# Loading all 128 partitions of every item in a chunked-attention stage, padding rows included

## The chip, the cores and the metric

The kernel runs on one core of one Trainium2 chip. The metric is the device time of one execution in microseconds (us). A single execution scatters by about 1% in these runs, so kernels are compared by the runs that were made side by side on one chip. Ratios are the mean time of one kernel's fast runs over the mean of the other's fast runs of the same rounds, with a 95% interval; so they are not quite the ratio of the medians quoted beside them. "Faster" or "slower" is given from 2% on, with the whole interval beyond it; a smaller difference whose interval leaves out 1 is called clear of noise.

## The reference

An attention stage (RWKV-5, 4 batches, 8 heads, 768 tokens, head dimension 48) is followed by a mixture of 8 experts:

```python
# attention: a running state per head
for t in range(S):
    y[:, :, t] = r_t @ (state + (u * k_t) outer v_t)
    state = w * state + k_t outer v_t
# experts: every token goes to one expert e (its own best, or that of the token before)
h = np.maximum(x[b, s] @ w1[e], 0.0)
out[b, s] = p[e] * (h @ w2[e])
```

All is fp32. The change touches only how the attention stage loads r, k and v.

## The kernel before: the parts that matter

The attention stage works through 16 items, one per batch and pair of heads. The tile `rk` holds r and k of both heads with the head dimension on the partitions: 48 rows of the first head, 16 rows of zeros, 48 rows of the second head, 16 rows of zeros. `vT` is laid out in the same way. `kv` holds tokens on the partitions and uses all 128 of them. Four sets of buffers take turns:

```python
NB = 4
ROWS = DP + DH                    # 64 + 48 = 112: the last 16 rows are zeros
...
def load(n):
    b, hp = divmod(n, HP)
    rk, vT, kv = rks[n % NB], vTs[n % NB], kvs[n % NB]
    q = slice(0, P if n < NB else ROWS)
    nc.sync.dma_start(out=rk[q].rearrange("p a c t -> p (a c t)"), in_=rk_d[b, hp, q])
    nc.sync.dma_start(out=kv, in_=kv_d[b, hp])
    nc.sync.dma_start(out=vT[q].rearrange("p a c t -> p (a c t)"), in_=vT_d[b, hp, q])
```

The first four items load every row, so that the padding in each buffer is zero once and for all; from item 4 on only rows 0 to 111 are loaded. The loop that uses them (cut; each helper issues the work of one item on several engines):

```python
for n in range(M + 2):
    if n + 2 < M:
        load(n + 2)
    turn(n - 2, ...)       # transposes tp, one item starts here on TensorE
    added(n); scale(n + 1) # VectorE kw, GpSimd ke, pd, rw; matmuls T
    inside(n - 1)          # matmuls yp, the last use of kv
    ...
    own(n); scores(n, 0); scores(n, 1)   # matmuls dp, sc
```

After every fourth item x is stored, and small matmuls for the expert logits (lp, then lq, called the gather) are added.

## Time and profile before

| | before |
|---|---|
| median of the runs beside the first comparison | 510.37 us (508.65 to 510.77, 4 runs) |
| profiled execution | 509.2 us |
| attention ends (last transposes tp start) | 137.08 us |
| TensorE idle between 25 and 125 us | 7.3 us, six times |
| time at half clock inside attention | 52.6 to 62.9 us |

The first three rows come from the runs and from the timeline of TensorE, the last two from the timeline and from the clock records. The prediction below shows the lines of the profile that carry its argument. One word on their reading: TensorE counts as busy from the start of a matmul to its modelled end. What tells of a lost microsecond is therefore the last column of the timeline, the idle before an instruction. "issue" there means that no semaphore explains the idle. Three words are used throughout: "the ring" stands for the loads that have been asked for and have not landed; a "block" is 256 instructions of TensorE in a row; a "crossing" is the start of the first instruction of a block.

### The profile page before, as it was taken

Reading aid. Unit: us, or ns where it says so; the run is one execution under the profiler, and the core shown is the slowest. Engines: PE = TensorE matmul, PEld = TensorE weight load, DVE = VectorE, ACT = ScalarE, POOL = GpSimd, SP = SyncE. Lnnn points to the kernel's source line nnn. Section 1 sums busy time; section 2 is a strip of 40 time slices with the busy share of each in tenths; the row PEclk is TensorE's granted clock in tenths of the full one; section 3 lists DMA queues with packets and bytes.
Section 4 is the critical chain, followed back from the end, with each engine's and each line's share of the span. In section 5 each row is a group of like instructions: output and inputs, shape, how many; then the busy total and the mean of one; then the engine's idle time right before and its main releaser. Section 6 shows DMA issues by size and latency. Waiting matters only on the chain.

```text
span 509.2 us, 8106 instructions
## 1 busy us (share of the span) xinstructions
PE 453.5 (89%) x3470; PEld 281.7 (55%) x3470; DVE 149.4 (29%) x243; ACT 73.0 (14%) x180; POOL 149.2 (29%) x133
## 2 busy tenths in 40 slices
PE   3989799899833589999999999999999999999980
PEld 2977598798623545555555555555555555555540
DVE  7776357566357010111110110111111111111020
ACT  2122122222200001011011110110111111011010
POOL 6876377482011250211311212212212202001111
PEclk9999599999965579999999999999999999999995
DMA  8999968841094130071071071071161152000001
GB/s 317 359 248 249 319 188 281 231 149 70 15 382 194 31 109 0 23 279 46 27 279 43 24 274 46 24 257 69 31 240 75 32 198 83 16 0 32 9 10 49
DMA packets 16525, 67.53 MB, mean 133 GB/s; under 512 B 2887, under 2 KB 6250, under 8 KB 14432
## 3 DMA queue, kind: packets, MB, share of 16 engines
q1 hardware_dynamic: 9504, 51.98, 30.3%
q0 software_dynamic: 3840, 10.23, 6.2%
q10 hardware_dynamic: 3136, 4.72, 2.7%
q8 instruction: 29, 0.48, 0.4%
q14 instruction: 16, 0.13, 0.1%
HBM read 57.48 MB, written 10.22 MB: 133 GB/s over the span
## 4 chain that ended last, share of the span: by engine, by line
issue 56%; PE 25%; POOL 13%; DMA 2%; POOLq 1%; DVE 1%; ACT 0%; SPq 0%
POOL out_dram L610 6%; PE sc L183 6%; POOL xg L566 5%; PE yp L194 5%; PE tp L216 3%; PE T L143 3%; PE dp L166 2%; PE mp L527 2%; PE T L154 2%; PE yp L204 2%; PE lp L227 1%; DMA x_d<-x 1%; DMA rk<-in_rk_dram 1%; PE lq L235 1%; DMA xg<-x_d,gid 1%
## 5 line engine op out<-in xcount | busy, mean ns | idle before, releaser
L594 PE MATMUL y<-hT,w2t 128*128 128x448 f32 x384 | 155.4, 541 | 0.0
L584 PE MATMUL h<-exT,w1t 128*128 128x448 f32 x384 | 155.0, 543 | 0.0
L584 PEld LDWEIGHTS h<-exT,w1t 128*128 128x128 f32 x384 | 71.9, 192 | 64.3 <-issue 64.3
L594 PEld LDWEIGHTS y<-hT,w2t 128*128 128x128 f32 x384 | 70.2, 190 | 58.8 <-issue 58.3
L610 POOL DMA_INDIRECT out_dram<-yo,sid x32 | 31.3, 978 | 174.6 <-DVE yo L608 174.0
L587 ACT ACTIVATE hT<-h 128x448 f32<-128x448 f32 x64 | 34.8, 544 | 284.8 <-PE h L584 284.8
L566 POOL DMA_INDIRECT xg<-x_d,gid x32 | 32.4, 1013 | 100.8 <-PE etp L578 84.7
L579 DVE COPY exT<-etp 128x384 f32<-128x384 f32 (+1 forms) x32 | 16.2, 508 | 131.9 <-PE etp L578 131.1
L608 DVE TENSOR_SCALAR yo<-otp,gate 128x384 f32<-128x384 f32 (+1 forms) x32 | 19.5, 615 | 118.7 <-PE otp L606 118.6
L183 PE MATMUL sc<-rw,kw 48*64 48x128 f32 x768 | 36.8, 292 | 2.7 <-issue 2.7
L127 POOL TENSOR_TENSOR ke<-kv,endT 128x576 f32<-128x576 f32 x16 | 26.1, 1634 | 27.1 <-DMA kv<-in_kv_dram 13.8
L183 PEld LDWEIGHTS sc<-rw,kw 48*64 48x64 f32 x768 | 31.0, 143 | 3.6 <-issue 3.5
L154 PE MATMUL T<-S,wd 48*64 48x64 f32 x256 | 30.3, 239 | 1.3 <-issue 1.1
L185 DVE TENSOR_TENSOR am<-sc,mask 128x768 f32<-128x768 f32 x32 | 29.3, 951 | 4.2 <-PE sc L183 3.8
L154 PEld LDWEIGHTS T<-S,wd 48*64 48x64 f32 x256 | 24.3, 143 | 6.8 <-issue 4.0
L129 POOL TENSOR_TENSOR pd<-rk 128x768 f32<-128x768 f32 x15 | 27.3, 1822 | 2.2 <-issue 2.2
L207 DVE TENSOR_TENSOR xT<-yp,own 128x768 f32<-128x768 f32 x16 | 15.3, 958 | 39.1 <-PE yp L204 39.1
L166 PE MATMUL dp<-pd,w_t 48*64 48x384 f32 x128 | 22.4, 521 | 4.7 <-issue 3.0
L130 POOL TENSOR_TENSOR rw<-rk,pw 128x768 f32<-128x768 f32 x15 | 25.3, 1688 | 3.3 <-PE yp L204 3.3
L194 PE MATMUL yp<-am,kv 128*64 128x128 f32 x384 | 26.2, 283 | 0.0
L578 PEld LDWEIGHTS etp<-ident,xg 128*128 128x128 f32 (+1 forms) x96 | 11.9, 150 | 21.9 <-issue 19.8
L156 ACT COPY S<-T 128x64 f32<-128x64 f32 x64 | 13.6, 213 | 71.0 <-PE T L154 71.0
(138 smaller groups left out, 312.5 us busy)
## 6 DMA issues: line engine op xcount, KB each, us to landing
w1t<-in_w_dram SPq DMA_DIRECT2D x8, 1536.0 KB, 6.3
w2t<-in_w_dram SPq DMA_DIRECT2D x8, 1536.0 KB, 7.6
kv<-in_kv_dram SPq DMA_DIRECT2D x16, 584.0 KB, 8.0
rk<-in_rk_dram SPq DMA_DIRECT2D x12, 672.0 KB, 10.4
x_d<-x ACTq DMA_DIRECT2D x4, 1152.0 KB, 6.0
vT<-in_vT_dram SPq DMA_DIRECT2D x12, 336.0 KB, 7.3
rk<-in_rk_dram SPq DMA_DIRECT2D x4, 768.0 KB, 8.4
vT<-in_vT_dram SPq DMA_DIRECT2D x4, 384.0 KB, 9.1
```

The source lines that it names most:

```text
L127: nc.gpsimd.tensor_mul(t["ke"], t["k"], spread(endT[:, hp].rearrange("p i d -> p (i d)"), 1, NCH))
L129: nc.gpsimd.tensor_mul(t["pd"], t["rT"], t["kT"])
L154: nc.tensor.matmul(t["T"][h * DP:(h + 1) * DP, c], lhsT=wd[q, t["hp"]], rhs=t["S"][q, c - 1], start=False, stop=True, skip_group_check=True)
L166: nc.tensor.matmul(dp[p * DP:(p + 1) * DP, h, :C2 * P].rearrange("p (c t) -> p c t", c=C2), lhsT=w_t[q, t["hp"], 1:2].to_broadcast([DH, DP ...
L183: nc.tensor.matmul(sc[z, h, c * P:(c + 1) * P], lhsT=t["kw"][q, 3 * g + c, z], rhs=t["rw"][q, 3 * g + c], start=True, stop=True)
L185: nc.vector.tensor_mul(t["am"][:, g], sc[:, :, :3 * P].rearrange("p h (c t) -> p h c t", t=P), spread(spread(mask, 1, 3), 1, 2))
L194: nc.tensor.matmul(t["y"][p * DP:(p + 1) * DP, h, c2 * P:(c2 + 1) * P], lhsT=t["v"][:, (2 * c + h) * DH:(2 * c + h) * DH + DP], rhs=t["am" ...
L566: nc.gpsimd.indirect_dma_start(out=xg[:n], out_offset=None, in_=x_d, in_offset=bass.IndirectOffsetOnAxis(ap=gid[:n, e * ST + j:e * ST + j ...
L584: nc.tensor.matmul(h[:, :CAP], lhsT=t[e]["w1"][:, m, kk, :], rhs=t[e]["xT"][:, kk, :], start=(kk == 0), stop=(kk == DK - 1))
L587: nc.scalar.activation(hT, h[:, :CAP], Act.Relu)
L594: nc.tensor.matmul(t[e]["y"][d][:, :CAP], lhsT=t[e]["w2"][:, m, d * P:(d + 1) * P], rhs=t[e][m], start=(m == 0), stop=(m == FK - 1))
L610: nc.gpsimd.indirect_dma_start(out=outs[c], out_offset=bass.IndirectOffsetOnAxis(ap=sid[:n, c:c + 1], axis=0), in_=yo[:n], in_offset=None, ...
```

## The change

The intent, as far as the edit tells it, is simplicity: one shape for all loads, at the price of 147 kB of zeros per item.

```diff
-        ROWS = DP + DH
 ...
-            q = slice(0, P if n < NB else ROWS)
-            nc.sync.dma_start(out=rk[q].rearrange("p a c t -> p (a c t)"), in_=rk_d[b, hp, q])
+            nc.sync.dma_start(out=rk.rearrange("p a c t -> p (a c t)"), in_=rk_d[b, hp])
             nc.sync.dma_start(out=kv, in_=kv_d[b, hp])
-            nc.sync.dma_start(out=vT[q].rearrange("p a c t -> p (a c t)"), in_=vT_d[b, hp, q])
+            nc.sync.dma_start(out=vT.rearrange("p a c t -> p (a c t)"), in_=vT_d[b, hp])
```

## The prediction

Passages of the recorded texts that told of the hardware what no trace and no run of this case shows are cut, and the cuts are marked. The rates that the forecast uses, 249 and 418 GB/s, are measured. No term of the sum is cut: 13.2 - 0.8 - 1.0 = 11.4 us, and 510.4 - 11.4 = 499.0 us. Where it speaks of the engine that fetches, the trace shows one of the 16 landings of a load behind the last of the other 15, by 1.7 to 2.7 us from 22 to 43 us; that this one fetches is the author's reading.

> **What bounds the kernel now**
>
> I read the page of the kernel before first. Its first 27% is the attention part (16 items, one per batch and pair of heads), then come routing and the experts. The change touches only the item loads of the attention part, so what it is worth must be read there. Lines: the span, TensorE's busy tenths, the granted clock, DMA share and rate in 40 slices of 12.7 us, and two load groups (KB, median us from issue to landing).
>
> ```profile
> span 509.2 us, 8106 instructions
> ...
> PE   3989799899833589999999999999999999999980
> ...
> PEclk9999599999965579999999999999999999999995
> DMA  8999968841094130071071071071161152000001
> GB/s 317 359 248 249 319 188 281 231 149 70 15 382 194 31 109 0 23 279 46 27 279 43 24 274 46 24 257 69 31 240 75 32 198 83 16 0 32 9 10 49
> ...
> rk<-in_rk_dram SPq DMA_DIRECT2D x12, 672.0 KB, 10.4
> ...
> rk<-in_rk_dram SPq DMA_DIRECT2D x4, 768.0 KB, 8.4
> ```
>
> To be seen: in slices 1 to 4 the 16 DMA engines are full, yet they carry 317 and 359 GB/s in the first two and 248 and 249 in the next two. In slice 5 the clock is at half. And the smaller (112-row) load lands later than the larger one. So next I cut that stretch into windows (busy us of PE, PEld, DVE, ACT, POOL with counts; then clock, DMA share, GB/s).
>
> ```profile
> 12.00:19.00 7.00, 7.00 (x89) 5.93 (x90) 6.12 (x7) 0.94 (x5) 7.00 (x5) 1.00 1.03 418
> ...
> 26.00:48.00 22.00, 19.27 (x444) 17.17 (x441) 16.62 (x17) 5.41 (x19) 17.52 (x11) 1.00 0.98 249
> 48.00:64.00 16.00, 12.98 (x194) 9.12 (x190) 5.27 (x6) 2.91 (x9) 5.09 (x4) 0.68 1.00 304
> 64.00:90.00 26.00, 25.90 (x587) 22.78 (x584) 17.81 (x20) 6.49 (x24) 19.41 (x12) 1.00 0.77 236
> ```
>
> Up to about 19 us only 128-row transfers move: 418 GB/s. From 26 to 48 us, rk and vT come with 112 rows: 249 GB/s at the same busy share. The engines are not idle; each packet takes longer. Then the same view cut at the items' beginnings on TensorE (the transposes tp in the chain of waits):
>
> ```profile
> 25.02:32.43 7.41, 6.36 (x143) 5.64 (x144) 5.65 (x7) 1.70 (x6) 7.41 (x6) 1.00 1.03 267
> 32.43:39.35 6.92, 6.31 (x144) 5.56 (x144) 5.16 (x5) 1.70 (x6) 4.35 (x3) 1.00 0.89 234
> 39.35:46.71 7.36, 6.29 (x143) 5.65 (x144) 5.50 (x6) 1.70 (x6) 5.82 (x5) 1.00 1.02 247
> 46.71:61.52 14.81, 11.79 (x176) 8.09 (x176) 6.56 (x8) 1.92 (x7) 5.87 (x4) 0.70 1.01 301
> 61.52:69.69 8.17, 8.17 (x156) 7.51 (x157) 3.70 (x5) 2.50 (x7) 5.02 (x3) 0.92 0.62 187
> ...
> 75.66:81.73 6.07, 6.07 (x143) 5.57 (x144) 4.41 (x6) 1.70 (x6) 4.80 (x4) 1.00 0.75 228
> ```
>
> A plain item takes 6.05 us when undisturbed (75.66), 7.84 with the logits matmuls (a later window, 111.25 to 119.09) and 7.51 with the gather (119.09 to 126.60). The early items take more. The timeline of PE shows where (last column: idle before, and its releaser):
>
> ```profile
> 31.44 0.77 PE L183 MATMUL sc<-rw,kw 48*64 48x128 f32 x19 [1.05 <-issue]
> ...
> 38.01 0.45 PE L183 MATMUL sc<-rw,kw 48*64 48x128 f32 x8 [0.61 <-issue]
> ...
> 44.95 0.77 PE L183 MATMUL sc<-rw,kw 48*64 48x128 f32 x20 [1.07 <-issue]
> ...
> 53.82 0.90 PE L166 MATMUL dp<-pd,w_t 48*64 48x384 f32 x1 [3.02 <-issue]
> ```
>
> PE waits on no tile there. Counting the trace's PE and PEld records up to each of these idles gives 705, 961, 1217, 1473, and for two later ones (1.06 us at 93.73, 0.48 at 100.37) 3009 and 3265: all whole multiples of 256 apart. The trace has one 16,384-byte packet on the queue marked "instruction" before each, ending at 30.10, 36.50, 43.54 and 52.31 us, and PE goes on 1.3 to 1.5 us after it. So TensorE runs out of instructions, because its own fetch comes late through the crowded DMA engines. From the crossing of one 256-block to the start of the fetch it triggers it took 4.6, 3.8, 4.2, 6.1 us in the 112-row stretch, but 1.9 at 17 us, where the engines were just as full of 128-row loads, and 0.3 to 1.3 in seven quiet cases. A block mostly lasts 5.4 to 6.0 us; fetch (1.2) and restart (1.4) leave about 3.4 us for the wait. The 3.02 us idle is followed, in the trace's clock records, by half clock from 52.6 to 62.9 us.
>
> [...]
>
> **The change part by part**
>
> No instruction moves: the issue order on every engine is the same, only the row count of the 24 loads of items 4 to 15 changes. Items 0 to 3 already load 128 rows.
>
> Added: 16 rows x (6144 + 3072) B = 147 kB per item, 12 times = 1.77 MB. An item is 1630 kB now and becomes 1778 kB. Removed: the 112-row shape. At the rates above an item's loads take 1630/249 = 6.55 us now, over the 6.05 us that TensorE needs; they will take 1778/418 = 4.25 us, below it, if the rate of the first four items holds. Four items with one store of x (1.18 MB, at about 367 GB/s from 67 ns per 1536-byte packet: 3.2 us) then need 20.2 us of the 27.4 us that TensorE works on them. The engines drain, and the fetches wait 1 to 2.5 us instead of 4 to 6: below the 3.4 us that hurt.
>
> What this gives back on TensorE, from the item windows less 6.05, 7.84 or 7.51: 1.36 + 0.87 + 1.31 + 6.97 + 0.66 + 1.37 (89.57 to 98.45, 8.88 long) + 0.67 (98.45 to 105.17, 6.72) = 13.2 us. Of it 7.3 are the six fetch idles, about 4.6 the half clock (14.81 - 3.02 - 7.84, and 0.66 behind it), the rest small waits.
>
> What I don't expect to get: 0.8 us in the first window, where POOL is busy all 7.41 us and hands over ke only just in time; and about 1.0 us of fetch idle that stays where a store of x, the loads and a fetch meet. 13.2 - 0.8 - 1.0 = 11.4 us. Routing and experts lie behind the end of attention and move forward whole. 510.4 - 11.4 = 499.0 us.
>
> **Rivals**
>
> - More bytes on full engines. If 249 GB/s is the rate of this stretch whatever the shape, 1.77 MB adds 7.1 us of DMA time, the fetches come later still: 515 to 518 us. For it: DMA share 0.98 to 1.03. Against: 418 GB/s at the same share in the same program, and kv, 128 rows in both, only slows when 112-row loads run beside it (181 ns per 4672-byte packet from 12 to 25 us, 245 from 38 to 51).
> - The loads quicken, but the fetch idles stay, because what delays a fetch is any full ring. The engine that fetches ends each load 2 to 4 us after the other 15 from 22 us on. For it: that lag begins with the first fetch, still among 128-row loads. Against: that fetch waited only 1.9 us. It would leave 505 to 510.
> - The idles shrink but one near the store at 48 us still drops the clock: some 4 us less gained, 503.
> - The load was never on the path: POOL waits 2.57, 1.54 and 6.48 us for kv, but PE never for POOL there. True of the data, so gains come through the fetch alone; were the fetch reading wrong, about 510.
>
> **Range and chances**
>
> All idles gone gives 497 to 498; one or two left with a clock drop, 503 to 505. Three runs of before spread 1.7 us[...]. So 499.0, range 495.5 to 505.5. Two per cent is 500.2, close to the centre: faster 0.60, same 0.35, slower 0.05.
>
> **What would show it**
>
> Right: 26 to 48 us at 290 to 420 GB/s with DMA share well below 0.98; rk with 768 KB landing in less than 10.4 us at the median; fetch idles before 125 us below 1.5 us in sum against 7.3; no half clock between 45 and 70 us; items of 6.0 to 6.3 us from the second window on; the end of attention some 11 us earlier, the rest as long as before. Wrong: a DMA share still near 1.0 at about 250 GB/s[...], or idles at multiples of 256 that stay although the share fell (the fetch reading falls).

## The result, and the profile after

| | before | after |
|---|---|---|
| median | 510.37 us (4 runs) | 501.33 us (501.00 to 503.03, 4 runs) |
| ratio | | 0.9836 [0.9804, 0.9868] |
| profiled execution | 509.2 us | 499.3 us |
| last transposes tp start | 137.08 us | 127.16 us |

The kernel moves more bytes and is 1.6% faster: by the 2% rule "same", but clear of noise. The time lies inside the predicted range; the gain is 9.0 us by the medians where 11.4 were forecast.

The page of the kernel after (the same rows as in the prediction):

```profile
span 499.3 us, 8106 instructions
...
PE   3999999999418499999999999999999999999980
...
PEclk9999999999755599999999999999999999999995
DMA  8989889430580310351250260170171061000001
GB/s 314 405 291 381 307 287 350 136 126 3 221 380 0 104 39 16 136 181 42 92 217 28 66 259 26 40 285 32 32 275 56 24 242 60 1 0 33 9 8 52
...
rk<-in_rk_dram SPq DMA_DIRECT2D x16, 768.0 KB, 7.4
```

Slices are 12.5 us here. The half-clock slice inside attention is gone; the one that remains (slices 11 to 14) belongs to routing, as before. A load of 768 KB now lands in 7.4 us at the median, sooner than one of 672 KB did (10.4). The windows of the kernel after, first by stretch, with the same columns as in the prediction:

```profile
12.00:19.00 7.00, 7.00 (x87) 5.85 (x85) 6.12 (x7) 1.07 (x5) 7.00 (x5) 1.00 1.03 418
...
26.00:48.00 22.00, 20.81 (x467) 18.09 (x462) 17.45 (x17) 5.12 (x18) 20.04 (x13) 1.00 0.91 327
48.00:64.00 16.00, 15.26 (x330) 12.88 (x334) 8.29 (x10) 4.57 (x15) 9.43 (x6) 1.00 0.88 317
64.00:90.00 26.00, 24.99 (x555) 21.64 (x546) 17.76 (x20) 6.70 (x23) 18.48 (x11) 1.00 0.85 303
```

From 26 to 48 us 327 GB/s move instead of 249. Averaged over the packet records of that stretch, a 6144-byte row of rk takes 255 ns instead of 406, and a 3072-byte row of vT 136 instead of 194. The DMA share however fell only from 0.98 to 0.91. Then the windows item by item:

```profile
24.05:30.13 6.08, 6.08 (x144) 5.58 (x144) 5.18 (x6) 1.71 (x6) 6.08 (x5) 1.00 0.86 304
30.13:36.79 6.66, 6.30 (x143) 5.56 (x144) 6.44 (x6) 1.71 (x6) 6.66 (x5) 1.00 0.86 293
36.79:43.61 6.82, 6.29 (x144) 5.66 (x144) 5.23 (x6) 1.71 (x6) 6.82 (x4) 1.00 0.97 364
43.61:52.45 8.84, 8.29 (x176) 5.83 (x176) 6.00 (x8) 1.92 (x7) 5.44 (x4) 1.00 1.02 385
52.45:60.66 8.21, 7.72 (x156) 7.13 (x157) 4.09 (x6) 2.44 (x7) 5.01 (x3) 1.00 0.88 320
...
80.55:89.28 8.73, 7.82 (x155) 7.09 (x156) 4.08 (x6) 2.44 (x7) 4.22 (x3) 1.00 0.84 325
```

The first item is at its undisturbed length (6.05 us). The next four are over theirs by 0.61, 0.77, 1.00 and 0.70 us, and the last one shown by 1.22 (it has the gather, so 7.51 is its measure). With the 0.03 of the first, and 0.03 elsewhere, 4.4 us remain of the 13.2 that the same windows of before held.

The first window begins 0.97 us earlier than in the kernel before (24.05 against 25.02), and this part is not the work of the loads: TensorE has no idle from 19 us up to there in either profile. At the start of both profiles TensorE ran at half speed, and it came to full speed at 21.9 us in the profile of before and at 19.4 in that of after. The same matmuls show it, before and then after:

```profile
19.50 2.19 PE L194 MATMUL yp<-am,kv 128*64 128x128 f32 x17
```

```profile
19.66 1.18 PE L191 MATMUL yp<-am,kv 128*64 128x128 f32 x17
```

(The clock column shows 1.00 from 12 to 19 us only because the records of the clock begin with that rise.) The moment varies from run to run of one kernel: in the second profile of the kernel after (run 12) it was 17.4 us. Over all profiles but that of run 7 it lies between 16.8 and 23.7 us, so it moves the time by up to some 3 us, an estimate from half of that spread. Differences of a microsecond between two single profiles should be read with this in mind.

TensorE's timeline says where the rest is lost:

```profile
35.46 0.45 PE L180 MATMUL sc<-rw,kw 48*64 48x128 f32 x8 [0.36 <-issue]
41.85 0.77 PE L180 MATMUL sc<-rw,kw 48*64 48x128 f32 x20 [0.53 <-issue]
48.25 0.53 PE L163 MATMUL dp<-pd,w_t 48*64 48x384 f32 x1 [0.55 <-issue]
54.47 1.53 PE L191 MATMUL yp<-am,kv 128*64 128x128 f32 x24 [0.49 <-issue]
```

With 0.91 us at 84.56 these are 2.84 us of idle instead of 7.29. Counting PE and PEld records up to them gives 961, 1217, 1473, 1729 and 3009: the same places in the program as before, multiples of 256 apart. So the fetch of instructions still comes late, only less so. Its waits, from the crossing of one 256-block to the start of the 16,384-byte instruction packet that the crossing triggers, in us (from the trace's records; the crossings at an idle are exact, the others are counted on from these):

```
block that begins at record   449   705   961  1217  1473  1729
before                       4.58  3.83  4.24  6.05  4.13  0.82
after                        3.22  4.00  3.90  3.98  3.78  3.79
```

### The profile page after: what moved, and what is told of

It is laid out like the page before. It is cut to its first block, busy times and chain, and to the rows that moved or that the text cites. A ratio compares the mean times of both kernels' runs of the same rounds, so it can differ in the third digit from the quotient of the medians.

```text
span 499.3 us, 8106 instructions
## 1 busy us (share of the span) xinstructions
PE 448.0 (90%) x3470; PEld 277.9 (56%) x3470; DVE 149.1 (30%) x243; ACT 73.0 (15%) x180; POOL 151.2 (30%) x133
## 4 chain that ended last, share of the span: by engine, by line
issue 56%; PE 25%; POOL 13%; DMA 2%; POOLq 1%; DVE 1%; ACT 0%; SPq 0%
POOL out_dram L607 6%; PE sc L180 5%; POOL xg L563 5%; PE yp L191 4%; PE tp L213 3%; PE T L140 2%; PE dp L163 2%; PE mp L524 2%; PE T L151 2%; PE yp L201 2%; DMA rk<-in_rk_dram 1%; DMA x_d<-x 1%; PE lp L224 1%; PE lq L232 1%; DMA xg<-x_d,gid 1%
## 5 line engine op out<-in xcount | busy, mean ns | idle before, releaser
L180 PE MATMUL sc<-rw,kw 48*64 48x128 f32 x768 | 34.4, 282 | 0.9 <-issue 0.9
L124 POOL TENSOR_TENSOR ke<-kv,endT 128x576 f32<-128x576 f32 x16 | 28.0, 1749 | 16.0 <-DMA kv<-in_kv_dram 6.8
L180 PEld LDWEIGHTS sc<-rw,kw 48*64 48x64 f32 x768 | 29.2, 138 | 1.4 <-issue 1.3
L151 PE MATMUL T<-S,wd 48*64 48x64 f32 x256 | 28.7, 233 | 1.1 <-issue 0.9
L151 PEld LDWEIGHTS T<-S,wd 48*64 48x64 f32 x256 | 22.6, 137 | 6.6 <-issue 3.6
L191 PE MATMUL yp<-am,kv 128*64 128x128 f32 x384 | 25.1, 276 | 0.5 <-issue 0.5
L575 PEld LDWEIGHTS etp<-ident,xg 128*128 128x128 f32 (+1 forms) x96 | 12.0, 151 | 21.9 <-issue 19.9
L575 PE MATMUL etp<-ident,xg 128*128 128x128 f32 (+1 forms) x96 | 16.7, 285 | 7.3 <-DMA xg<-x_d,gid 7.2
```

The source lines that it names most:

```text
L124: nc.gpsimd.tensor_mul(t["ke"], t["k"], spread(endT[:, hp].rearrange("p i d -> p (i d)"), 1, NCH))
L151: nc.tensor.matmul(t["T"][h * DP:(h + 1) * DP, c], lhsT=wd[q, t["hp"]], rhs=t["S"][q, c - 1], start=False, stop=True, skip_group_check=True)
L180: nc.tensor.matmul(sc[z, h, c * P:(c + 1) * P], lhsT=t["kw"][q, 3 * g + c, z], rhs=t["rw"][q, 3 * g + c], start=True, stop=True)
L191: nc.tensor.matmul(t["y"][p * DP:(p + 1) * DP, h, c2 * P:(c2 + 1) * P], lhsT=t["v"][:, (2 * c + h) * DH:(2 * c + h) * DH + DP], rhs=t["am" ...
L575: nc.tensor.transpose(tp[:, kk, :n], t[e]["xg"][j][:n, kk * P:(kk + 1) * P], ident[:n, :n])
```

## The experiments

Twelve kernels ran. Three of the successful ones compute a wrong result on purpose; in these the fallback for overfull experts is switched off, so that wrong data cannot send the program down another path. Their outputs held NaN, and only their times and traces are used.

**1. The bytes of before in the shape of after.** From item 4 on 128 rows, but only 7/8 of each row.

```diff
+            m = 8 if n < NB else 7
-            nc.sync.dma_start(out=rk.rearrange("p a c t -> p (a c t)"), in_=rk_d[b, hp])
+            nc.sync.dma_start(out=rk.rearrange("p a c t -> p (a c t)")[:, :m * 192], in_=rk_d[b, hp][:, :m * 192])
 # likewise vT with m * 96
```

> 128 rows, but only 7/8 of each row from item 4 on, so exactly the bytes of before (wrong result on purpose: part of k and v stays stale; the fallback for overfull experts is switched off). Shape theory[...]: as fast as the kernel after or a little faster, 499.5 to 502 us, and a 5376-byte packet takes about 220 ns. Bytes theory (the gain or loss comes from the amount moved): like before, 509 to 511 us.

Measured: 502.05 us (498.36 to 503.76, 4 runs), ratio 0.9856 [0.9776, 0.9936]; a 5376-byte packet took 226 ns between 26 and 48 us. The same bytes, in another shape, take less time than before, clear of noise: the shape of the loads decides, not the amount. The median is at the upper edge of what was expected. In its profile the first four item windows are at their floor (6.07, 6.08, 6.07, 7.84 us), and one idle of 1.95 and one of 0.42 us are left.

**2. All 128 rows as two loads of 64.**

```diff
+            cut = [slice(0, P)] if n < NB else [slice(0, DP), slice(DP, P)]
-            nc.sync.dma_start(out=rk..., in_=rk_d[b, hp])
+            for q in cut:
+                nc.sync.dma_start(out=rk[q]..., in_=rk_d[b, hp, q])
 # likewise vT
```

> All 128 rows of rk and vT, but as two loads of 64 rows each from item 4 on: bytes and row sizes of the kernel after. [...]a 6144-byte packet takes 400 ns or more instead of 254, the fetch idles come back (5 us or more before 125 us) and the time is 507 to 515 us. Rival (the number 112 itself is bad[...], and 64, a power of two, is as good as 128): like after, 500.5 to 503 us.

Measured: 521.7 us (520.23 to 526.11, 6 runs), ratio 1.0226 [1.0164, 1.0287], slower than both kernels, clear of noise, and slower than expected. The window of the same stretch:

```profile
26.00:48.00 22.00, 16.77 (x353) 14.93 (x355) 11.97 (x12) 4.39 (x15) 12.87 (x8) 0.92 1.02 226
```

226 GB/s at a DMA share of 1.02, with 433 ns per 6144-byte packet; 12 us of TensorE idle between 20 and 120 us, and three stretches of half clock inside attention (granted clock 0.92 from 26 to 48 us, 0.87 from 64 to 90). The rows, their size and the bytes are those of the kernel after; only their grouping into loads differs. Slow packets and idles came as expected, and the rival (the number 112 is bad, 64 as good as 128) falls. Why loads of 64 rows are slow is not shown. One rival is left that no run tests: there are now twice as many loads of rk and vT, and kv, still one load of 128 rows, slows too (335 ns for its 4672-byte packet against 226 in the kernel after).

**3. No item loads after the first four.**

```diff
+            if n < NB:
                 nc.sync.dma_start(out=rk..., in_=rk_d[b, hp])
                 nc.sync.dma_start(out=kv, in_=kv_d[b, hp])
                 nc.sync.dma_start(out=vT..., in_=vT_d[b, hp])
```

> No item is loaded after the first four; the items compute on old data (wrong result on purpose, fallback off). If the idles of TensorE at multiples of 256 instructions come from the crowd of loads, all of them vanish, the fetch waits under 1.3 us, and the time is the floor: 501.3 less the 4.4 us that the item windows of after still show over their undisturbed lengths, 496.5 to 498 us. If they belong to the instruction stream itself, 500.5 to 503 us as after.

Measured: 498.03 us (497.13 to 498.56, 4 runs), ratio 0.9779 [0.972, 0.9839]. TensorE has no idle between 20 and 122 us, and every item window is at its floor. The fetches of the blocks between 23 and 58 us waited at most 0.8 us, but for 2.9 beside the store of x (crossings by count), where in the kernel after they waited 3.2 to 4.0. So the loads are what delays them. The time is just above the 496.5 to 498 us expected. The difference is what all item loads together cost the kernel after: some 3 us.

**4. The crowd without the data.** Every item computes on the data of items 0 and 1; the 14 later loads go to buffers that nobody reads.

```diff
-            rk, vT, kv = rks[n % NB], vTs[n % NB], kvs[n % NB]
+            g = n if n < 2 else 2 + n % 2
+            rk, vT, kv = rks[g], vTs[g], kvs[g]
             # ... the three loads ...
+            rk, vT, kv = rks[n % 2], vTs[n % 2], kvs[n % 2]
```

> The compute works on the data of the first two items only, and all other item loads (128 rows) go to buffers that nobody reads (wrong result on purpose, fallback off): the crowd without any wait for data. Loads then run back to back until about 60 to 65 us. Fetch theory: TensorE still idles at multiples of 256 instructions, 0.3 to 1 us each, while loads run, and no longer after; 498.5 to 502 us. Data theory (it idles because a tile is late): no idle, 496.5 to 498 us.

Measured: 500.87 us (one run, state unknown). The windows from 26 to 48 us, of the kernel without loads and then of this one:

```profile
26.00:48.00 22.00, 21.90 (x523) 19.81 (x523) 19.22 (x19) 5.53 (x20) 21.96 (x14) 1.00 0.15 54
```

```profile
26.00:48.00 22.00, 21.31 (x471) 18.45 (x467) 16.36 (x17) 5.23 (x19) 18.62 (x12) 1.00 1.02 410
```

The idles of TensorE in this one:

```profile
41.89 0.77 PE L182 MATMUL sc<-rw,kw 48*64 48x128 f32 x20 [0.29 <-issue]
48.06 0.53 PE L165 MATMUL dp<-pd,w_t 48*64 48x384 f32 x1 [0.32 <-issue]
54.20 1.53 PE L193 MATMUL yp<-am,kv 128*64 128x128 f32 x24 [0.40 <-issue]
```

No tile that TensorE uses waits for a late load here, and yet it idles, at the same three instructions as in the kernel after. Data that come late are ruled out as the cause of these. They sum to 1.01 us, where the same three are 1.57 us in the kernel after and its five 2.84; the profile is of a single run. And a number falls out: in a ring kept full by 128-row loads the fetches of six blocks waited 3.4, 3.6, 3.7, 3.7, 3.7 and 3.1 us. A wait of 3.7, the packet's 1.1 and the restart's 1.4 make 6.2 us per 256 instructions, an estimate, where a plain stretch of TensorE's work takes 5.4 to 6.0.

**5 and 6. One load of the two at a time.** In the kernel before, rk alone or vT alone is loaded with 128 rows.

```diff
-            nc.sync.dma_start(out=rk[q]..., in_=rk_d[b, hp, q])     # run rk_full
+            nc.sync.dma_start(out=rk..., in_=rk_d[b, hp])
-            nc.sync.dma_start(out=vT[q]..., in_=vT_d[b, hp, q])     # run vT_full
+            nc.sync.dma_start(out=vT..., in_=vT_d[b, hp])
```

> One part of the change alone: rk with 128 rows, vT still with 112. If each 112-row load slows mainly itself, two thirds of the gain: 503 to 506 us, a 6144-byte packet near 260 to 300 ns. If one odd shape in the ring is enough[...], most of the loss stays: 506 to 510 us, 6144-byte packets of 128-row loads above 320 ns.

> The other part alone: vT with 128 rows, rk still with 112. Each for itself: one third of the gain, 506 to 509 us, 3072-byte packets near 140 to 165 ns. One odd shape is enough: 508 to 511 us, as before.

Measured: rk alone 503.65 us (502.41 to 506.02, 4 runs), ratio 0.9894 [0.9851, 0.9937]; vT alone 508.49 us (507.77 to 509.61, 4 runs), ratio 0.9989 [0.9959, 1.002]. With rk alone, 6144-byte packets took 296 ns and 294 GB/s moved from 26 to 48 us; with vT alone the 3072-byte packets took 155 ns while rk's stayed at 383. So each shape mainly slows its own packets. But time does not divide with the bytes: vT alone gives nothing that can be told from zero, and its profile still has an idle of 2.19 us and 6.8 us of half clock from 53.3 us, while that of rk alone has neither.

**7. Three buffers, done wrongly.**

```diff
-        NB = 4
+        NB = 3
```

> The kernel after with three buffers of each item tile instead of four: fewer loads stand in the ring when a fetch comes. If the backlog sets the fetch's wait, the waits between 25 and 60 us fall from 3.2 to 4.0 us to below 3, the idles go, and the time is 498 to 501 us. If loads then come too late for GpSimd and TensorE waits for tiles instead, 503 us or more.

Measured: 880.33 us and a wrong result, ratio 1.7268. With three buffers the load of item n + 2 was recorded ahead of the last use of item n - 1 in the same buffer, so the program as written asked for the wrong data. That sent it into the fallback (13,207 instructions in the profile instead of 8,106). It says nothing about the question; run 11 is its correct form.

**8. 120 rows.**

```diff
-        ROWS = DP + DH
+        ROWS = 120
```

> The kernel before with 120 rows instead of 112: [...]6144-byte packets stay at 350 ns or more and the time is 506 to 516 us. Row-count theory (112 is odd, more rows are simply better): halfway, 503 to 507 us, packets near 300 ns.

Measured: 518.53 us (512.56 to 520.55, 4 runs), ratio 1.014 [1.0072, 1.0208]. More rows than 112, and slower still. Its profiled run is counted as slow (over 1.5% above the fastest run of the kernel) and left out of the ratio, so its packet times (446 ns from 26 to 48 us) are only an indication. The trace has 1032 packets of 4 bytes on this queue instead of 1056, one fewer for each of the 24 loads; read as 15 engines taking part instead of 16, this is the author's inference. Row count as such ("nearer to 128 is better") falls; that one engine fewer alone explains the loss is not excluded by this run.

**9 and 10. Fewer instructions, the loads untouched.** The two half-width score matmuls of a pair become one of full width, in the kernel after and in the kernel before.

```diff
-                for i in range(2):
-                    for h in range(2):
-                        q, z = slice(h * DP, h * DP + DH), slice(i * DP, (i + 1) * DP)
-                        nc.tensor.matmul(sc[z, h, ...], lhsT=t["kw"][q, 3 * g + c, z], rhs=..., ...)
+                for h in range(2):
+                    q = slice(h * DP, h * DP + DH)
+                    nc.tensor.matmul(sc[:, h, ...], lhsT=t["kw"][q, 3 * g + c], rhs=..., ...)
```

> The kernel after with the two half-width score matmuls of each pair merged into one of 128 columns: the same products, 24 matmuls and 24 weight loads fewer of 144 each per item, and no load changed. A block of 256 instructions then lasts an item's 6.05 us times 256/240 or more, some 6.4 us, longer than the 6.2 us that a fetch needs in a full ring. Fetch theory: the idles at multiples of 256 go (2.8 us now, below 0.8 then) although the loads are as dense as before; 498 to 500 us if the score matmuls take as long as now. Rival (the idles belong to late data or to PSUM): they stay, 501 to 503 us; if the merged form is slower on TensorE itself, items of over 6.2 us show it.

> The same edit on the kernel before, 112-row loads kept. Fetch theory: fewer instructions, fewer and shorter idles; [...]500 to 506 us. If the slow loads themselves (data late) set the time, it stays at 508 to 511 us.

Measured: after with merged scores 512.74 us (511.76 to 516.03, 4 runs), ratio 1.0051 [0.9979, 1.0123]; before with merged scores 511.25 us (509.26 to 515.83, 4 runs), ratio 1.0043 [0.9968, 1.0117]. As times, both missed: the merged form is slower on TensorE itself, 6.79 us per plain item instead of 6.05, so some 0.7 us for each of 16 items. As a test they are the clearest of all. From 26 to 48 us, after and then before:

```profile
26.00:48.00 22.00, 22.00 (x382) 18.74 (x378) 16.89 (x18) 5.31 (x19) 19.78 (x12) 1.00 0.83 308
```

```profile
26.00:48.00 22.00, 22.00 (x388) 18.88 (x386) 17.00 (x17) 5.95 (x20) 18.68 (x11) 1.00 0.92 250
```

Neither has a single idle of TensorE between 20 and 120 us. In the second the 112-row loads crawl at 250 GB/s as ever, 370 ns per 6144-byte packet, and every item up to there is 6.79 us long, as in the first. Here a block of 256 instructions lasts some 7.2 us (6.79 x 256/240, an estimate), longer than the 6.2 us estimated from run 4 for its fetch, and the shape of the loads cost nothing. One reservation: the slower item, 6.79 us, also leaves more room for an item's loads (6.55 us by the prediction's sum).

**11 and 12. Three buffers, done rightly, beside the kernel after.**

```diff
-        NB = 4
+        NB = 3
 ...
-            if n + 2 < M:
-                load(n + 2)
             ...
                 inside(n - 1)
+            if n + 2 < M:
+                load(n + 2)
```

> The three-buffer kernel done correctly: the earlier one asked for an item's load before the last use of the buffer it goes to was recorded, so it computed on wrong data. Here the load is recorded after that use. If fewer loads in the ring shorten the fetch's wait, idles below 1 us in sum and 498 to 501 us, 1 to 3 us below the kernel after in the same call. If loads come too late for GpSimd, TensorE waits for ke or pd, some 1 us per item: 505 us or more.

> The kernel after once more, with more rounds, to set the size of its gain and to compare the three-buffer kernel with it on the same chip: 501 to 502.5 us, 0.983 to 0.985 of before, fetch idles of 2 to 4 us before 125 us and no half clock between 45 and 70 us.

Measured: three buffers 498.67 us (497.62 to 501.86, 6 runs), ratio to before 0.9771 [0.9731, 0.9811], result correct; the kernel after 503.34 us (501.23 to 505.60, 6 runs), ratio 0.9857 [0.9816, 0.9897]. Three buffers take less time than both kernels, clear of noise, and stand within a microsecond of the kernel that loads nothing (ratios to before 0.9771 and 0.9779). The stretch from 26 to 48 us with three buffers:

```profile
26.00:48.00 22.00, 22.00 (x507) 19.88 (x506) 17.86 (x18) 6.13 (x21) 17.74 (x11) 1.00 0.97 366
```

TensorE is busy throughout, while 366 GB/s move, more than in the kernel after. The waits of the six blocks fell to 3.5, 2.0, 0.9, 1.8, 3.2 and 2.0 us, and one idle of 0.35 us is left before 120 us. Why they fell is not shown. At these crossings two to four loads were under way, in the kernel after three or four, so the number alone does not sort the waits: with three under way a fetch waited 0.9 to 3.5 us here and 3.9 to 4.0 in the kernel after, and run 4, with four to seven, had 3.1 to 3.7. The edit also asks for each load later in the loop, and four buffers with the late load were not tried. The second run of the kernel after lies a little above the 501 to 502.5 us expected, and otherwise confirms the first: five idles, 3.42 us in sum, at the same counts, and no half clock inside attention.

## Why the prediction was right, and where its size was off

**The bound was named rightly.** Fetch idles and the clock drop that follows the longest of them were what the loads cost. Runs 3, 4, 9 and 10 show it: no idles without loads, idles without late data, no idles with slow loads, and the shape's effect gone together with the idles.

**The rate was nearly right.** 1778 kB at the rate of the first four items, 418 GB/s, was the forecast for an undisturbed ring. Run 4, with a ring kept full, moves 410 GB/s between 26 and 48 us. In the kernel after, 327 GB/s at a share of 0.91 make some 360 at a full share: the 6144-byte packets took 255 ns against 239 from 12 to 19 us, but those of kv 226 against 181. So one reading in the prediction was wrong: kv does not slow only when 112-row loads run beside it. Its two figures there (181 and 245 ns) also belong to windows 10.5 us earlier than written; from 12 to 25 and from 38 to 51 us of the span the trace gives 206 and 299. The first rival (more bytes on full engines, 515 to 518 us) is refuted by the result and by run 1.

**That the shape sets the rate held its test**: 64 rows at a time are slow with the very same rows (433 ns per 6144-byte packet against 255, run 2), and 128 rows with the bytes of before are not (226 ns per 5376-byte packet, run 1). What in the hardware makes a shape slow is not shown.

**The clock went as forecast**: no half clock between 45 and 70 us after the change, and with it the estimated 4.6 us of before were gone. That the idle brings the drop is read from their order in time. No threshold is shown: an idle of 1.95 us (run 1) passed without a drop, those of 2.02 us (run 2), 2.19 us (run 6) and 3.02 us (before) did not, and in the slow profile of run 8 half clock came 0.8 us after one of 1.50 us. In run 9 the clock fell for 3.4 us from 64.6 us with no idle at all, beside the gather's matmuls of 9 columns; why is open.

**The step that failed in size**: "The engines drain, and the fetches wait 1 to 2.5 us instead of 4 to 6". They wait 3.2 to 4.0 us between 23 and 58 us, and 4.8 once beside a store of x. Two things were wrong with it. The 1.9 us came from the fetch at 17 us, whose crossing no idle marks; the position was counted back from later ones, and one sample was made a rule. The same first fetch waited 1.9 us in the kernel after and in run 4 too, so it is not like the later ones, and why is open. Run 4 measured the later situation six times: 3.1 to 3.7 us in a full ring. So the second rival, that any full ring delays a fetch, was half right. And the engines did not drain as the sum of bytes had it: the sum made 20.2 us of 27.4, a share of 0.74, and 0.91 was measured from 26 to 48 us. Faster loads and earlier freed buffers let the queue ask for the next load sooner (13 times between 26 and 48 us against 11 before). The term "about 1.0 us of fetch idle that stays" was therefore 2.84 us of idle, 4.4 us in the item windows. The 0.8 us held back for GpSimd's ke was wrong the other way: that window kept 0.03. So 13.2 less 4.4 makes 8.8 us, and with the 0.97 us of the earlier rise of the clock 9.8 us, against 9.9 that attention ended earlier in this pair of profiles. The 0.97 is luck of the pair; the 8.8 is to be compared with the 11.4 forecast, and 9.0 is the difference of the medians.

**What was expected of the profile**: bandwidth (327), landing time (7.4 us) and clock came as written. Three did not: the DMA share was 0.91, not well below 0.98; the idles summed to 2.84 us, not below 1.5; and the items from the second window on took up to 6.82 us, not 6.0 to 6.3. Attention ended 9.9 us earlier, not 11, and the rest took 372.1 us in both, as forecast.

**The chances**: 0.60 had been put on more than 2%. The measured 1.6% is on the other side of that line, by an amount (1.1 us) that the mis-sized term covers.

## What to carry to other kernels

Leaving padding rows out of the loads saved nothing here: 112 rows moved at 249 GB/s at a DMA share of 0.98, where 128 rows had reached 418 at 1.03. Look at the rate that the odd shape gets at a full DMA share before counting its bytes. If TensorE idles with no tile to wait for, count its records between the idles; a multiple of 256 pointed here to its instruction fetch, which waited 3.2 to 4.0 us beside the loads of the kernel after and, without loads (run 3), at most 0.8 us, but for 2.9 beside a store. Faster loads alone helped only in part here. The idles went with fewer instructions per microsecond, which saved no time in sum (runs 9 and 10), and nearly went with three buffers and later loads, which saved 4.7 us more.
